# Blocks 8 to 11 as one group of four in an attention and two-layer kernel: second layer by seven products, weights' sums placed earlier, start and end reordered

## The chip, the cores and the metric

The kernel runs on one core of a Trainium2 chip. The metric is device time in microseconds (us) of one execution, the median over several runs. Everything below that names an engine uses the profile's short names: PE is TensorE (matrix products; PEld is its loading of weights), DVE is VectorE, ACT is ScalarE, POOL is GpSimd, SP is SyncE, which here only issues transfers.

## The reference

A sliding-window attention whose scores decay with distance is followed by a normalisation and two matrix layers with a residual. B, H, S, D are 8, 8, 576 and 64; the model width is 512, the hidden width 2048. The kernel computes in half precision with single-precision sums.

```python
scores = scale * np.matmul(q, k.transpose(0, 1, 3, 2))
...
bias = slopes[:, None, None] * (-np.abs(rel).astype(np.float32))[None, :, :]
mask = (rel >= 0) & (rel < window)          # window = 128
scores = np.where(mask, scores + bias[None], -1000000000.0)
...
attn = attn / (np.sum(attn, axis=-1, keepdims=True) + 1e-09)
x = np.matmul(attn, v)                      # then heads side by side: B, S, H * D
mu = np.mean(x, axis=-1, keepdims=True)
var = np.mean((x - mu) ** 2, axis=-1, keepdims=True)
xn = (x - mu) / np.sqrt(var + 1e-06) * g_ln
ch = np.maximum(xn @ w_ch1, 0.0) @ w_ch2
return (x + ch).astype(np.float32)
```

## The kernel before, in words

**Blocks and groups.** Two batches make a pair, and the tokens of a pair are cut into nine blocks of 128 tokens (the ninth, T, holds the two tails of 64). Four pairs give 36 blocks, numbered 0 to 35 in `order`. Attention runs block by block. The two layers run over groups of consecutive blocks: `GROUPS` says how many blocks each group has, six groups of two and then six of four (line 26). A group's input is the normalised x of its blocks, transposed, in one tile `xT`; its hidden values lie in one tile `ht`.

**Attention steps.** The list `steps` (lines 654 to 705) holds small pieces of attention. From block 8 on, each block n has four: (1) the values of block n (`values`, two halves on TensorE, each followed by a reciprocal and a scaling on VectorE, lines 473 to 510) and the scores of block n+2 (`attend`, matmuls and one exponential on ACT per half, lines 407 to 449); (2) the masks of block n+2 (two multiplications on VectorE, line 454) and the statistics of block n (`stats`: two instructions on VectorE, then two on GpSimd that give the reciprocal deviation, lines 536 to 542); (3) `turn`, the transposing of queries and keys for a later pair of blocks: for the first three pairs TensorE transposes into the banks of the scores and VectorE and ACT copy out (lines 326 to 336), for the last a transfer does it; (4) `normal`, which centres and scales block n on VectorE and then has SP issue a transposing transfer into `xT` (lines 522 to 534). Loads from memory are issued on GpSimd's queue, ahead of the values (`load_until`, lines 266 to 271); GpSimd's two arithmetic instructions of a block stand in the same queue.

**First layer.** `mlp1` (lines 719 to 750) has 16 units; a unit is four matmuls into one bank and one rectification on ACT (on VectorE for the units listed in `on_dve`). With two blocks a matmul has 256 columns, with four 512.

**Second layer, two ways.** `mlp2` (lines 752 to 772) is the plain way: 16 matmuls of 512 columns per block, summed in one bank, which `finish` adds to x on VectorE (line 903) and stores. `fast_mlp2` (lines 798 to 898), for groups from `FAST` on, splits hidden, weights and output into quarters and computes the group by seven products instead of eight. It needs sums of quarters of the weights, made once by `combine_w2` (lines 178 to 192, eight instructions on VectorE, the last two of which overwrite weights that the plain way reads), and sums of quarters of hidden, made for each group by `combine_hidden` (lines 783 to 796): four instructions after the first layer's unit 10, four more within the products. Each product is 8 matmuls of 256 columns for each of two pairs of blocks; eight additions (`add`, line 845) gather the products, and `send` stores a pair of blocks. A product's bank can be written again only after its addition.

**Banks.** Four banks of the accumulator serve the layers and the values; two double ones serve the scores and the transposes. From the fast groups on the four are a `ring` handed out in turn (`psum`, lines 377 to 385); within `fast_mlp2` two are set aside and two (`others`) serve the values, the second product and the last.

**What sets the order.** The order on TensorE, SP, ACT and VectorE is that of the program text, written by hand: `weave_at` (lines 926 to 930) runs the units of a layer and, after unit u, as many attention steps as u stands in its list of places; after the units in `also` it emits one of the eight weights' sums. The lists are at lines 947 to 966. An instruction that waits holds up all that follow on its engine. Before the first layer begins, single warm products (`warm`, lines 278 to 283) fill TensorE's time.

Of the kernel before, what the change touches and what calls it, by code (L numbers as in the profile page):

```python
# [24 lines left out]
HALF = P // 2  # L25
GROUPS = [2] * 6 + [4] * 6
FAST = 6

# [31 lines left out]
def kernel(  # L60
# [246 lines left out]
    def turn(p, i, in_sc=False, copies=(nc.vector.tensor_copy, nc.scalar.copy)):  # L307
# [19 lines left out]
        if i < 4:  # L327
            transposed("q", p, i, [t[:, 0] for t in ps])
            transposed("k", p, i, [t[:, 1] for t in ps])
            for b, copy in enumerate(copies):  # L330
                copy(out=q[:, b], in_=ps[b][:, 0])
                copy(out=k[:, b].rearrange("p h (c r) -> p r h c", r=2), in_=ps[b][:, 1])
        else:
            for tag, t, dst, copy in zip("qk", ps, (q, k), copies):
                transposed(tag, p, i, [t[:, 0]])
                copy(out=dst[:, 0].rearrange("p h (c r) -> p r h c", r=2), in_=t[:, 0])
# [288 lines left out]
    def turn_step(n, *how):  # L625
        p, blk = order[n]
        return [(turn, p, blk // 2) + how]
# [22 lines left out]
    def warm_step(n):  # L650
        return [[(warm, n)]]
# [4 lines left out]
    steps += values_steps(0)  # L656
    steps += [turn_step(2, True, (nc.scalar.copy, nc.scalar.copy))]
    steps += values_steps(1) + warm_step(4)
# [33 lines left out]
    for n in range(8, count):  # L692
# [4 lines left out]
        if n + 2 < count:  # L697
            step += scores_step(n + 2)
        steps.append(step)
        steps.append(  # L700
            [m for t in (n + 1, n + 2) if t < count for m in masks_of(t)] + [(stats, n)]
        )
        if n + 1 < count:
            steps.append(turn_at(n + 1))
        steps.append([(normal, n)])
    combined = combine_w2()
# [11 lines left out]

    def mlp1(g, on_dve=()):
        xT = turned_x[g]  # L720
        w = w1 if g < FIRST_GROUPS else w1g
        cols = len(members[g]) * P
        ht = hidden[g] = hidden_pool.tile([P, NFB, 4 * P], FP16, tag="ht", name="ht")
        turn_about = chain(*zip(range(QF), range(QF, NFB)))
        for u, fb in enumerate(turn_about if g >= FAST else range(NFB)):
# [21 lines left out]
            yield cols  # L747
            if g >= FAST and u == 10:
                for i in range(4):
                    combine_hidden(g, 0, i)  # L750
# [47 lines left out]
    def fast_mlp2(g):  # L798
# [77 lines left out]
        add("z", 0, 1, False)  # L876
        send(0)
        yield DM
        yield from product("x", s[2], t3, False)
        add("x", 1, 0, True)  # L880
        add("x", 1, 1, False)
        if use["w"][0] is use["w"][1]:
# [6 lines left out]
        else:  # L889
            low, high = slice(0, QD), slice(QD, DM)  # L890
            last = product("w", a[1][1], t4, True)
            send(1, cols=high, queues=(nc.sync, nc.scalar))
            yield DM
# [50 lines left out]
    with tc.manual_schedule(engines={engine.PE, engine.SP}):  # L944
        with tc.manual_schedule(engines={engine.Activation, engine.DVE}):
# [4 lines left out]
            weave_at(mlp2(1), 0, 1, 2, 3, 4, 6, 6)  # L950
            weave_at(mlp1(2), 0, 3, 3, 6, 8, 11)
            weave_at(mlp2(2), 0, 2, 4, 6, 7)


            weave_at(mlp1(3, (9, 10, 11)), 8, 8, 12, 13)
            weave_at(mlp2(3), 0, 1, 1, 3, 4, 4, 5, 6)
            weave_at(mlp1(4), 0, 4, 8, 10, 10, 14)
            weave_at(mlp2(4), 0, 2, 2, 5, 5, 7, also=(1, 4, 6))
            weave_at(mlp1(5), 0, 5, 5, 8, 10, 12, also=(3, 6, 9))
            weave_at(mlp2(5), 0, 1, 2, 4, 6, 7)  # L960
            ring += [ps_mm.tile([P, DM], FP32, tag="mm", name="ps_r") for _ in range(4)]
            for g in range(6, len(GROUPS)):
                weave_at(
                    mlp1(g), 0, 2, 5, 7, 8, 10, 13, 15, also=(1, 4) if g == 6 else ()
                )
                weave_at(fast_mlp2(g), 1, 3, 6, 7, 7, 10, 12, 13)
# [31 lines left out]
```

## Time and profile before

| what | us |
|---|---|
| three runs | 318.67, 319.58, 320.78 |
| median | 319.58 |
| the profiled execution, its own time | 320.09 |
| its span in the profile | 318.3 |
| first layer of blocks 8 and 9 begins | 96.18 |
| their plain second layer begins | 106.84 |
| first layer of blocks 10 and 11 begins | 116.68 |
| their plain second layer begins | 126.93 |
| first layer of blocks 12 to 15 begins | 136.82 |
| their seven products begin | 153.18 |
| last matmul's record ends, last issue of a store, span ends | 313.4, 315.24, 318.3 |

The profile is of one execution; its span is the time from the first to the last instruction, and the execution's own time holds some more around it. A group of the profile stands under a line of the kernel, an engine and an operation, with the tiles written and read. Of the matmuls the starts are exact and the ends modelled, so the pace of a row of them is read from the starts. Times inside the span count from its start.

### The profile page before, as it was taken

The page shows a single profiled execution, that of the slowest core. Times are in us where ns is not written, and L with a number is a line of the kernel's source. Part 1 is how long each engine was busy: PE and PEld are TensorE (multiplying, and loading weights), DVE is VectorE, ACT ScalarE, POOL GpSimd, SP SyncE. Part 2 cuts the span into 40 slices and gives each one's busy share as a digit, 9 for nine tenths or more (in the row PEclk, how much of TensorE's full clock was granted, in tenths as well). Part 3 has the DMA queues.
Part 4 walks back from the last instruction along what each step waited for, and adds up shares of the span by engine and source line. Part 5 has one row for each costly group of instructions (what it writes and reads, how often), then busy time and mean ns, then how long its engine had stood idle before and what let it go on. Part 6 is the DMA issues. An engine that isn't in the chain of part 4 may idle for free.

```text
span 318.3 us, 9920 instructions
## 1 busy us (share of the span) xinstructions
PE 304.7 (96%) x4190; PEld 205.4 (65%) x4190; DVE 228.9 (72%) x547; ACT 179.4 (56%) x311; POOL 124.7 (39%) x196
## 2 busy tenths in 40 slices
PE   7789999999898999999999999999999999999993
PEld 3468755757656657555885588558855874784583
DVE  2769977878667699767995889469948995761462
ACT  6578774757647558459437832772487247305600
POOL 8922769557245365483345472240001001100000
PEclk9989999999999999999999999999999999999999
DMA  9999999999986979499949994893347244015005
GB/s 112 165 206 197 190 151 182 198 110 146 106 95 91 116 87 161 52 153 62 77 51 146 181 124 52 134 156 64 83 91 127 18 84 85 19 36 114 0 0 135
DMA packets 121183, 34.68 MB, mean 109 GB/s; under 512 B 112049, under 2 KB 116785, under 8 KB 121138
## 3 DMA queue, kind: packets, MB, share of 16 engines
q0 software_dynamic: 89216, 18.36, 70.5%
q1 hardware_dynamic: 31602, 15.42, 25.6%
q8 instruction: 33, 0.54, 0.7%
q10 hardware_dynamic: 320, 0.26, 0.4%
q14 instruction: 12, 0.10, 0.1%
HBM read 36.90 MB, written 9.44 MB: 146 GB/s over the span
## 4 chain that ended last, share of the span: by engine, by line
PE 84%; DVE 5%; POOL 3%; ACT 2%; DMA 2%; issue 2%; POOLq 0%; ACTq 0%
PE ps_r L728 26%; PE ps_r L827 23%; PE ps_m L761 11%; PE ps_m L728 10%; PE ps_sc L434 5%; PE ps_r L487 3%; PE ps_sc L301 2%; PE ps_pv L487 2%; ACT probs L443 2%; DMA k<-in_k_dram 2%; POOL q L237 1%; DVE o L903 1%; DVE x L496 1%; PE ps_warm L283 1%; DVE probs L454 1%
## 5 line engine op out<-in xcount | busy, mean ns | idle before, releaser
L728 PEld LDWEIGHTS <-w1g 128*128 128x128 f16 x640 | 60.4, 98 | 50.5 <-DVE x L496 1.8
L728 PE MATMUL ps_r<-xT,w1g 128*128 128x512 f16 x384 | 85.1, 379 | 0.0
L443 ACT ACTIVATE probs<-ps_sc 128x1024 f16<-128x1024 f32 x56 | 54.2, 1021 | 52.3 <-PE ps_sc L434 52.3
L744 ACT ACTIVATE ht<-ps_r 128x512 f16<-128x512 f32 x96 | 56.2, 600 | 31.6 <-PE ps_r L728 31.5
L761 PE MATMUL ps_m<-w,ht 128*128 128x512 f16 x192 | 46.0, 380 | 1.2 <-ACT ht L744 1.2
L539 POOL TENSOR_TENSOR rstd<-moments,powers 128x1 f32<-128x1 f32 x28 | 6.8, 243 | 102.4 <-DVE moments L585 102.4
L827 PE MATMUL ps_r<-w,ht 128*128 128x256 f16 x384 | 44.1, 273 | 0.0
L454 DVE TENSOR_TENSOR probs<-probs,m 128x1024 f16<-128x1024 f16 x56 | 37.5, 688 | 8.7 <-ACT probs L443 8.5
L247 POOL DMA_DIRECT2D vx<-in_v_dram x40 | 34.7, 884 | 22.3 <-PE ps_r L487 9.0
L827 PEld LDWEIGHTS <-ht 128*128 128x128 f16 x384 | 37.1, 98 | 4.8
L744 ACT ACTIVATE ht<-ps_m 128x256 f16<-128x256 f32 x91 | 32.9, 391 | 8.6 <-PE ps_m L728 6.2
L728 PE MATMUL ps_m<-xT,w1g 128*128 128x256 f16 x256 | 31.5, 273 | 2.2 <-DVE x L496 0.9
L761 PEld LDWEIGHTS <-ht 128*128 128x128 f16 x192 | 17.1, 98 | 18.7 <-issue 1.3
L237 POOL DMA_DIRECT2D q<-in_q_dram x30 | 20.5, 692 | 19.3 <-PE ps_sc L301 10.6
L584 DVE BATCH_NORM_STATS2 st<-x 128x6 f32<-128x512 f16 x36 | 24.6, 685 | 0.0
L237 POOL DMA_DIRECT2D k<-in_k_dram x30 | 20.2, 686 | 4.8 <-DMA w<-in_moe_w_ch_dram 3.5
L434 PE MATMUL ps_sc<-q,k 64*64 64x128 f16 (+1 forms) x1088 | 20.5, 210 | 1.5 <-ACT probs L443 1.1
L827 PE MATMUL ps_r<-w,hs 128*128 128x256 f16 x192 | 21.9, 273 | 0.0
L487 PEld LDWEIGHTS <-probs 128*128 128x128 f16 x448 | 18.8, 97 | 4.7 <-DVE probs L454 0.3
L827 PEld LDWEIGHTS <-hs 128*128 128x128 f16 x192 | 18.8, 98 | 2.2
L845 DVE TENSOR_TENSOR o<-ps_r,x 128x512 f32<-128x512 f32 x24 | 16.5, 686 | 4.3 <-PE ps_r L827 4.3
L434 PEld LDWEIGHTS <-k 64*64 64x64 f16 x1088 | 15.2, 108 | 6.8 <-issue 4.6
(87 smaller groups left out, 381.4 us busy)
## 6 DMA issues: line engine op xcount, KB each, us to landing
out_dram<-o SPq DMA_DIRECT2D x68, 128.0 KB, 2.9
k<-in_k_dram POOLq DMA_DIRECT2D x32, 128.0 KB, 6.0
vx<-in_v_dram POOLq DMA_DIRECT2D x32, 128.0 KB, 6.0
w<-in_moe_w_ch_dram POOLq DMA_DIRECT2D x8, 512.0 KB, 9.4
q<-in_q_dram POOLq DMA_DIRECT2D x24, 128.0 KB, 4.2
q<-in_q_dram POOLq DMA_DIRECT2D x24, 64.0 KB, 3.8
k<-in_k_dram POOLq DMA_DIRECT2D x8, 64.0 KB, 4.8
vx<-in_v_dram POOLq DMA_DIRECT2D x8, 64.0 KB, 5.0
```

Of the source, the lines that this page charges most:

```text
L237: nc.gpsimd.dma_start(out=t[b * n // 2 : (b + 1) * n // 2], in_=src[2 * p + b, :, i * P : i * P + n, :].rearrange("h (c r) d -> c h r d", ...
L247: nc.gpsimd.dma_start(out=vx[p0 : p0 + n, :, 0:D], in_=v[b, :, t0 : t0 + n, :].rearrange("h p d -> p h d"),)
L434: nc.tensor.matmul(in_halves(ps[cols, j, n, t, :])[:, r, queries], kt[rows, hp, cols], in_halves(qt[rows, b, hp])[:, r, queries], start=Tr ...
L443: nc.scalar.activation(out=dst.rearrange("p (n j) q -> p j n q", j=2), in_=ps.rearrange("p j n t q -> p j n (t q)"), func=AF.Exp, scale=in ...
L454: nc.vector.tensor_tensor(out=dst, in0=dst, in1=mask, op=ALU.mult)
L487: nc.tensor.matmul(ps[:, i, :], pr[:, h, t, :], vext[(p * NSLOT + o) % NV][:, h, :], start=(n == 0), stop=(n == len(terms) - 1),)
L584: nc.vector.bn_stats(out=st, in_=xs[order[n]])
L728: nc.tensor.matmul(ps[:, 0:cols], w[:, kb, fb * P : (fb + 1) * P], xT[:, kb, 0:cols], start=(kb == 0), stop=(kb == NKB - 1),)
L744: nc.scalar.activation(out=ht[:, fb, 0:cols], in_=ps[:, 0:cols], func=AF.Relu)
L761: nc.tensor.matmul(sums[at], ht[:, fb, at * P : (at + 1) * P], w2[:, fb, :], start=(fb == 0), stop=(fb == NFB - 1),)
L827: nc.tensor.matmul(banks[name][pair][:, pair, :], lhs[:, fb, pair * P : (pair + 1) * P], rhs[:, fb, :], start=(first and fb == 0 and (pair ...
L845: nc.vector.tensor_tensor(out=o[:, at, cols], in0=banks[name][at.start][:, at, :], in1=(x if to_x else o)[:, at, cols], op=ALU.add,)
```

## The change

`GROUPS` becomes four groups of two and seven of four, and `FAST` goes from 6 to 4: blocks 8 to 11, two groups before, are one group. Its first layer runs in two halves, each over two blocks with matmuls of 256 columns, the halves writing the two sides of one hidden tile; sums of hidden are taken after unit 10 of the second half. Its second layer is the seven products.

The 24 attention steps that lay around the two groups' layers lie around the new group's: 5 in the first half, 7 in the second, 12 in the products (the other groups of four have 8 and 8). For block 11 (`HURRIED`) the statistics come before the masks and the centring before the transposing of queries and keys.

The eight weights' sums move: one into the first layer of blocks 4 and 5, two into their second, one into the first layer of blocks 6 and 7, two into their second, and two into the first half of the new group. Before, they lay in the layers of blocks 8 to 11 (six) and in the first layer of blocks 12 to 15 (two).

At the start, two warm products go before the transposes of block 2 and three between its queries' and its keys'. At the end, the last group's first send alternates between the queues of SP and ACT; in all fast groups the addition of the second pair's high columns comes before that of its low columns, and in the last group the store of the high columns stands between them.

The diff:

```diff
-GROUPS = [2] * 6 + [4] * 6
-FAST = 6
+GROUPS = [2] * 4 + [4] * 7
+FAST, HURRIED = 4, 11
...
             transposed("q", p, i, [t[:, 0] for t in ps])
+            if p == 0 and i == 1:
+                warm(3)
             transposed("k", p, i, [t[:, 1] for t in ps])
...
-    steps += [turn_step(2, True, (nc.scalar.copy, nc.scalar.copy))]
+    steps += warm_step(2) + [turn_step(2, True, (nc.scalar.copy, nc.scalar.copy))]
...
-        steps.append(
-            [m for t in (n + 1, n + 2) if t < count for m in masks_of(t)] + [(stats, n)]
-        )
-        if n + 1 < count:
-            steps.append(turn_at(n + 1))
-        steps.append([(normal, n)])
+        to_mask = [m for t in (n + 1, n + 2) if t < count for m in masks_of(t)]
+        turns = [turn_at(n + 1)] if n + 1 < count else []
+        if n == HURRIED:
+            steps += [[(stats, n)] + to_mask, [(normal, n)], *turns]
+        else:
+            steps += [to_mask + [(stats, n)], *turns, [(normal, n)]]
...
-    def mlp1(g, on_dve=()):
+    def mlp1(g, on_dve=(), part=0, parts=1):
...
-        cols = len(members[g]) * P
-        ht = hidden[g] = hidden_pool.tile([P, NFB, 4 * P], FP16, tag="ht", name="ht")
+        cols = len(members[g]) * P // parts
+        if part == 0:
+            hidden[g] = hidden_pool.tile([P, NFB, 4 * P], FP16, tag="ht", name="ht")
+        xT, ht = (t[:, :, part * cols : (part + 1) * cols] for t in (xT, hidden[g]))
...
-            if g >= FAST and u == 10:
+            if g >= FAST and part == parts - 1 and u == 10:
...
-        send(0)
+        send(0, queues=(nc.sync, nc.scalar) if g == len(GROUPS) - 1 else (nc.sync,))
         yield DM
         yield from product("x", s[2], t3, False)
+        add("x", 1, 1, False)
+        low, high = slice(0, QD), slice(QD, DM)
+        if g == len(GROUPS) - 1:
+            send(1, cols=high, queues=(nc.sync, nc.scalar))
         add("x", 1, 0, True)
-        add("x", 1, 1, False)
...
-            low, high = slice(0, QD), slice(QD, DM)
             last = product("w", a[1][1], t4, True)
-            send(1, cols=high, queues=(nc.sync, nc.scalar))
...
-            weave_at(mlp1(2), 0, 3, 3, 6, 8, 11)
-            weave_at(mlp2(2), 0, 2, 4, 6, 7)
-            weave_at(mlp1(3, (9, 10, 11)), 8, 8, 12, 13)
-            weave_at(mlp2(3), 0, 1, 1, 3, 4, 4, 5, 6)
-            weave_at(mlp1(4), 0, 4, 8, 10, 10, 14)
-            weave_at(mlp2(4), 0, 2, 2, 5, 5, 7, also=(1, 4, 6))
-            weave_at(mlp1(5), 0, 5, 5, 8, 10, 12, also=(3, 6, 9))
-            weave_at(mlp2(5), 0, 1, 2, 4, 6, 7)
+            weave_at(mlp1(2), 0, 3, 3, 6, 8, 11, also=(14,))
+            weave_at(mlp2(2), 0, 2, 4, 6, 7, also=(3, 5))
+            weave_at(mlp1(3, (9, 10, 11)), 8, 8, 12, 13, also=(5,))
+            weave_at(mlp2(3), 0, 1, 1, 3, 4, 4, 5, 6, also=(2, 6))
             ring += [ps_mm.tile([P, DM], FP32, tag="mm", name="ps_r") for _ in range(4)]
-            for g in range(6, len(GROUPS)):
-                weave_at(
-                    mlp1(g), 0, 2, 5, 7, 8, 10, 13, 15, also=(1, 4) if g == 6 else ()
-                )
+            weave_at(mlp1(4, (), 0, 2), 0, 3, 5, 10, 13, also=(2, 8))
+            weave_at(mlp1(4, (), 1, 2), 0, 0, 4, 8, 10, 12, 15)
+            weave_at(fast_mlp2(4), 0, 3, 4, 5, 7, 7, 7, 8, 10, 11, 12, 13)
+            for g in range(5, len(GROUPS)):
+                weave_at(mlp1(g), 0, 2, 5, 7, 8, 10, 13, 15)
                 weave_at(fast_mlp2(g), 1, 3, 6, 7, 7, 10, 12, 13)
```

## The prediction

> **What bounds the kernel now.** I read the page first, then the chain of waits in order of time, then TensorE's and VectorE's timelines around blocks 8 to 11, the busy times by stage, and the queues at both ends. The page:
>
> ```profile
> span 318.3 us, 9920 instructions
> PE 304.7 (96%) x4190; PEld 205.4 (65%) x4190; DVE 228.9 (72%) x547; ACT 179.4 (56%) x311; POOL 124.7 (39%) x196
> PE 84%; DVE 5%; POOL 3%; ACT 2%; DMA 2%; issue 2%; POOLq 0%; ACTq 0%
> ```
>
> TensorE sets the end; from 137 us on the chain holds nothing else but the last addition. The chain in order of time (start, length, what):
>
> ```profile
> 96.02 0.57 POOL rstd L542
> 96.61 0.41 DVE xc L526
> 97.15 0.42 DVE x L496
> 97.77 0.28 issue
> 98.04 0.75 DVE o L903
> 98.84 1.03 PE ps_m L728 x8
> ...
> 107.00 2.59 PE ps_m L761 x12
> ...
> 301.14 12.24 PE ps_r L827 x112
> ```
>
> Where the first layer of blocks 8 and 9 begins, TensorE waits for VectorE, whose queue stands behind GpSimd's reciprocal deviation. The last two lines price the second layer: 2.59/12 = 0.216 us per plain product of 512 columns, and 12.24 us for the 112 of seven products. Busy times by stage:
>
> ```profile
> core 0: us, PE busy (x) PEld busy (x) DVE busy (x) ACT busy (x) POOL busy (x), PEclk, DMA share, GB/s
> 136.80:152.70 15.90, 15.90 (x188) 7.94 (x186) 11.14 (x25) 12.88 (x21) 10.13 (x16) 1.00 1.34 106
> 152.70:168.40 15.70, 15.70 (x305) 13.85 (x306) 15.23 (x33) 5.59 (x8) 6.00 (x11) 1.00 0.84 67
> ```
>
> First layer, then seven products, of the first fast group (blocks 12 to 15). In the products VectorE is busy 15.23 of 15.70 us and still holds nobody up; it carries eight steps of attention there. Its timeline gives the price of its instructions by their starts, 0.60 each, 0.72 and 0.10 for statistics:
>
> ```profile
> 155.14 0.69 DVE L845 TENSOR_TENSOR o<-ps_r,x 128x512 f32<-128x512 f32 x1
> 155.75 0.68 DVE L796 TENSOR_TENSOR w<-ht,hs 128x1024 f16<-128x1024 f16 x1
> 156.35 1.29 DVE L454 TENSOR_TENSOR probs<-probs,m 128x1024 f16<-128x1024 f16 x2
> 157.55 0.69 DVE L584 BATCH_NORM_STATS2 st<-x 128x6 f32<-128x512 f16 x1
> 158.27 0.18 DVE L585 BATCH_NORM_AGGREGATE moments<-st 128x2 f32<-128x6 f32 x1
> ```
>
> The ends: granted clock by stretch, and the last issues of the two queues.
>
> ```profile
> 11.05:14.47 3.42, 1.83 (x79) 1.40 (x80) 2.81 (x10) 0.41 (x2) 3.07 (x6) 1.00 2.00 161
> 14.47:17.88 3.41, 3.41 (x29) 1.47 (x29) 2.11 (x8) 2.78 (x5) 2.12 (x4) 0.50 1.23 199
> 17.88:21.29 3.41, 2.33 (x81) 1.89 (x74) 1.87 (x5) 3.08 (x4) 1.15 (x2) 1.00 1.24 207
> ```
>
> ```profile
> 310.63 3.03 SPq L922 DMA_DIRECT2D out_dram<-o  x5
> 313.70 0.77 SPq L918 DMA_DIRECT2D out_dram<-o  x1
> 314.57 0.55 SPq L922 DMA_DIRECT2D out_dram<-o  x1
> 315.24 0.55 SPq L918 DMA_DIRECT2D out_dram<-o  x1
> ```
>
> After 14.47 us the clock is half for 3.41 us. At the end five issues stand in one queue, so the last comes at 315.24 though its data is ready at 313.83.
>
> **The change part by part.** All times are of the profiled execution.
>
> *Second layer.* 64 products of 512 columns (13.81) become 112 of 256 (12.24): **-1.57**. The first layer keeps its 128 matmuls of 256 columns. Its waits change: before, 0.51, 0.12 and 0.10 at 117.64 to 118.74 (banks held by a plain sum), 0.14 at 122.5, and 0.41 and 0.47 behind ACT's two exponentials; after, only the last kind, once per half: **-0.93**. Bounds 0 and -1.75.
>
> *Weights' sums sooner*, eight of 0.60 on VectorE. One falls into its wait of 1.74 us before 66.80, two into 0.28 and 1.00 before 73.19 and 74.89, one into 1.67 before 81.37: nothing, and with that cover gone 0.6 each. The fifth and sixth fall between 91.8 and 98.8, the chain shown above: the fifth delays the statistics of block 10, GpSimd's answer, and the values of block 11; the sixth stands before L903, which frees the fourth bank. The first layer's fourth unit starts at 100.03 instead of 98.84: **+1.19**. Bounds 0 (if GpSimd's wait of 0.95 and a bank more took them) and 1.2. The last two stand in the first half.
>
> *Second half's input.* Block 11's x is centred after its statistics (100.72), two masks (101.92), a weights' sum (102.52): done at 102.85. SP issues its DMA transpose about 0.1 later. Such a transpose took 2.4 to 7.4 us to land; block 11's took 6.0 (102.20 to 108.24), with the q and k loads in flight that GpSimd sends right after the same reciprocal deviation, as it will. So it lands at 109.0. TensorE is through the first half at 106.84 + 1.19 = 108.0: **+1.0**, bounds 0 (the median of 3.8) and 2.5. Before, this input had until 116.7.
>
> *VectorE in the products.* The stage gets twelve steps of attention in place of eight. From the copy of block 17's queries, which TensorE releases at 114.9 (without the 1.0), VectorE has no free place up to the last product's addition: 8 sums of hidden (5.2), 8 additions (4.8), 6 masks (3.6), values of blocks 14 to 16 at 1.1 (3.3), 3 statistics at 0.82 (2.46), 4 centrings at 0.33 (1.3), copies of queries and keys (0.63 + 2 x 0.95), and the GpSimd answer for block 15, whose centring stands right behind its statistics (0.95); with 0.2 for a product not yet done it is 24.4 us, to 139.3. On the way the values of block 15 wait for the bank of the second product, the scores of 17 for a bank that VectorE copies out. Before, from the fourth unit (98.84) to the second unit of the next group (137.68) TensorE took 38.84 us, 1.75 of it the waits above; 38.84 - 1.75 - 1.57 = 35.5 us of work are left. From 100.03 on, with two ACT waits (0.82) and the 1.0, it would reach that unit at 137.4; but the unit needs the last addition's bank, free at 139.4 + 1.0 = 140.4: **+3.0**. Bounds 0 (the stage before hid 15.23 in 15.70) and 4.0 (GpSimd's longest, 1.86, in place of 0.95). I take 3.0, as VectorE's queue is summed from its own rows. The middle is 140.4 - 137.7 = **+2.7**.
>
> *Order in moved steps.* Eight stores of blocks 8 to 11, 0.6 us each on SP, now come at the end of the products and ahead of block 16's and 17's transposes, which TensorE needs over 15 us later: nothing, and 4.8 if it did. Loads keep their order on GpSimd. The swapped additions cost nothing where all groups but the last are concerned, as nobody waits between them.
>
> *Start.* Two warm products before block 2's transposes and three between its q and k fall into waits of 0.42, 0.23 and 0.79 for loads; k lands at 13.83 in any case. They add 1.08 us to a stretch with 1.83 busy; 2.33 was enough at 17.88. So the clock stays, and four warm products end at 15.4 instead of 16.2. Then ACT's copies bind: block 0's copy at 16.5, the first exponential at 17.1 instead of 18.21: **-1.1**. The first quarter of weights landed at 18.03, the next at 20.54 and 23.07, each before its use even so. Bounds -1.2 and +0.7 (five at 427 ns less the waits' 1.44).
>
> The Trainium skill (TensorE: Matmul & The Clock Gate, What's actually happening) says that the clock is gated by a free-running window of 3413 ns that a kernel's start does not reset. The 3.41 us above agree in length; no run here shows another phase. By that rule a median execution may not have had the slow stretch at all, and this term would be 0, and the time 321.4.
>
> *End.* Half of the first send goes to ACT's queue, and the addition for the high columns comes first, done at 312.35. Each queue then has four issues at 0.62 to 0.69 as ACT's had (312.98, 313.60, 314.29, 314.94): the last at about 314.4 instead of 315.24: **-0.85**, bounds -1.0 (data ready at 313.83) and 0. The landing about 2 us later stays.
>
> Sum: -1.57 - 0.93 + 1.19 + 1.0 + 3.0 - 1.1 - 0.85 = +0.74. The profiled execution took 320.09 us (its span 318.3 and 1.8 around it, which nothing here changes), 0.51 over the median of 319.58; 320.09 + 0.74 = 320.8, and by the median **320.3**.
>
> **Rivals.**
> - *VectorE holds nobody up in the products* (the 3.0 goes, the rest stays): 320.3 - 3.0 = 317.3. For it: the stage before hid 97% busy. Against: twelve steps instead of eight.
> - *The saving comes whole* (1.19 and 1.0 go too): 317.3 - 2.2 = 315.1. Against: the chain at 96 to 98.8 has no place for two sums.
> - *The change does not do at the start what it says:* the clock falls all the same, or was up already: 320.3 + 1.1 = 321.4. For it: the three times shown differ by 2.1 us. The Trainium skill's free-running window (TensorE: Matmul & The Clock Gate, What's actually happening) would do this.
> - *Slower:* the transpose of block 11, behind the loads, decides. Each us over 6.0 from issue to landing is a us of TensorE's. At 7.4, the longest shown, the time is 321.7; slower by over 1% from 8.5. For it: the queue's landings of 6.0 and 7.4 came beside loads; against: the median of 3.8.
>
> **How the numbers follow.** A measurement of this kernel can hardly tell less than 1% (3.2 us) from no change: faster is under 316.4, slower over 322.8. Forecast as summed 0.47 (own range 319.1 to 321.7); VectorE keeps up 0.17; whole saving 0.06; no gain at the start 0.15; late transpose 0.15. Faster: the whole saving and a corner of the first rival, 0.08. Slower: the transpose's upper half and the forecast's tail, 0.10. Same: 0.82. The range from 316.9 to 322.4 leaves out the whole saving, the lower edge of the first rival, and the slower cases, 0.2 in all.
>
> **What would show it.** Right: granted clock 1.00 from 4.2 us on and the first exponential near 17.1; TensorE's fourth unit of the first half waiting for L903; a wait for xT at the second half; VectorE over 97% busy in blocks 8 to 11's products and TensorE waiting there and at the next group's second unit for L845; the last issue 0.9 us sooner after the last product. Wrong: no TensorE wait between 108 and 140 us, or the next fast group's start earlier than before by over 2 us.

## The result, and the profile after

| | us |
|---|---|
| after, median of 22 runs (lowest to highest) | 321.47 (320.14 to 324.13) |
| before, median of 22 runs on the same chip | 319.57 (318.26 to 321.85) |
| ratio | 1.0060, 95% interval 1.0042 to 1.0078 |
| profiled execution of after, and its span | 321.24, 319.5 |

The change costs 0.6%, 1.9 us. The two profiled executions differ by 1.15 us (321.24 and 320.09), since that of before lies 0.5 us above its median and that of after 0.2 below. Line numbers after the change are some four higher (a sum's addition is L849, the plain way's addition L908, a plain first-layer matmul L732, a product's L831).

The page of after: TensorE is 1.5 us less busy, VectorE 5.9 us more, and VectorE's share of the chain that ended last went from 5% to 11%.

```profile
span 319.5 us, 10054 instructions
...
PE 303.2 (95%) x4243; PEld 210.2 (66%) x4243; DVE 234.8 (73%) x559; ACT 179.8 (56%) x311; POOL 125.1 (39%) x196
...
PE 76%; DVE 11%; POOL 3%; DMA 3%; ACT 3%; issue 3%; DVEq 0%; POOLq 0%; ACTq 0%
```

Busy times by stage in after: the two stretches at the start whose second had a granted clock of 0.50 before, then the products.

```profile
core 0: us, PE busy (x) PEld busy (x) DVE busy (x) ACT busy (x) POOL busy (x), PEclk, DMA share, GB/s
11.05:14.47 3.42, 2.40 (x56) 1.10 (x59) 3.06 (x10) 0.56 (x1) 3.06 (x5) 1.00 2.02 166
14.47:17.88 3.41, 3.24 (x84) 2.02 (x84) 2.13 (x9) 3.00 (x6) 2.12 (x3) 1.00 1.25 205
119.13:139.17 20.04, 17.43 (x372) 14.49 (x369) 18.45 (x41) 8.65 (x11) 9.29 (x17) 1.00 1.08 98
```

TensorE's timeline in after (start, length, line, count, and in brackets the idle time in front and who ended it):

```profile
97.71 1.16 PE L732 MATMUL ps_r<-xT,w1g 128*128 128x256 f16 x8 [1.78 <-DVE x L498]
99.51 1.47 PE L732 MATMUL ps_r<-xT,w1g 128*128 128x256 f16 x12 [0.65 <-DVE o L908]
...
107.06 2.78 PE L732 MATMUL ps_r<-xT,w1g 128*128 128x256 f16 x24 [0.25 <-ACT ht L748]
...
124.43 0.64 PE L489 MATMUL ps_r<-vx,probs 128*128 128x65 f16 x16 [0.35 <-DVE o L849]
...
126.00 0.41 PE L436 MATMUL ps_sc<-q,k 64*64 64x128 f16 x16 [0.58 <-DVE k L334]
...
137.31 1.02 PE L732 MATMUL ps_r<-xT,w1g 128*128 128x512 f16 x4 [0.85 <-DVE o L849]
139.17 1.02 PE L732 MATMUL ps_r<-xT,w1g 128*128 128x512 f16 x4 [0.83 <-DVE o L849]
```

The bracket understates what a wait costs, as the ends of matmuls are modelled. By the starts (the distance to the matmul before, less the usual pace of 0.110 us for 256 columns and 0.216 for 512) the rows lose 1.94, 0.81, 0.41, 0.51, 0.78, 1.05 and 1.00 us; such losses are meant below. The last four, 3.34 us, are TensorE waiting for VectorE within and right after the products. In before TensorE waits nowhere for VectorE from 119 us on. The first layer's second half (from 107.5 on) waits for no input. VectorE's timeline at the end of the products shows why the last two wait:

```profile
134.58 0.68 DVE L456 TENSOR_TENSOR own<-own,m 128x1024 f16<-128x1024 f16 x1
135.19 0.68 DVE L586 BATCH_NORM_STATS2 st<-x 128x6 f32<-128x512 f16 x1
135.90 0.18 DVE L587 BATCH_NORM_AGGREGATE moments<-st 128x2 f32<-128x6 f32 x1
136.00 0.66 DVE L849 TENSOR_TENSOR o<-ps_r,o 128x512 f32<-128x512 f32 x1
136.58 0.68 DVE L849 TENSOR_TENSOR o<-ps_r,x 128x512 f32<-128x512 f32 x1
137.18 0.41 DVE L333 COPY q<-ps_sc 128x512 f16<-128x512 f16 x1
137.51 0.72 DVE L334 COPY k<-ps_sc 128x512 f16<-128x512 f16 x1
138.12 0.40 DVE L528 TENSOR_SCALAR xc<-x,moments,rstd 128x512 f16<-128x512 f16 x1
138.43 0.68 DVE L849 TENSOR_TENSOR o<-ps_r,o 128x512 f32<-128x512 f32 x1
```

No idle time stands in front of any of these rows: VectorE works without a pause, and the last addition, which frees a bank of the next group, comes after masks, statistics, copies and a centring of attention. Its product was long ready: the last matmul of it starts at 135.12, 3.3 us ahead of the addition.

The last issues of SP and of ACT in after, one fence each:

```profile
314.36 0.60 SPq L923 DMA_DIRECT2D out_dram<-o  x1
315.06 0.54 SPq L927 DMA_DIRECT2D out_dram<-o  x1
315.70 0.54 SPq L923 DMA_DIRECT2D out_dram<-o  x1
```

```profile
314.39 0.85 ACTq L923 DMA_DIRECT2D out_dram<-o  x1
315.34 0.56 ACTq L927 DMA_DIRECT2D out_dram<-o  x1
316.00 0.55 ACTq L923 DMA_DIRECT2D out_dram<-o  x1
```

The last matmul starts at 314.57 (before 313.10), so the last issue follows it by 1.43 us instead of 2.14.

Between the two profiles the time went so: start -0.67 (first layer from 20.13 instead of 20.81), middle +2.16 (the next fast group's second unit at 139.17 instead of 137.68, over and above the start), nothing from there to the last matmul, end -0.3. The gain at the end stands in the other profiles too: from the last matmul's start to the end of the span it takes 4.6 to 4.9 us in the ten usable profiles with the changed end, and 5.2 to 5.4 in the three without.

One disturbed execution each of steps_later (616.5 us) and of copies_sums (325.73 us) is left out of the medians below, and as that of steps_later is the profiled one, only the times of that kernel are used.

### The profile page after: what moved, and what is told of

The parts are those of the page before. It is cut to its first block, busy times and chain, and to the rows that moved or that the text cites. A ratio compares the mean times of both kernels' runs of the same rounds, so it can differ in the third digit from the quotient of the medians.

```text
span 319.5 us, 10054 instructions
## 1 busy us (share of the span) xinstructions
PE 303.2 (95%) x4243; PEld 210.2 (66%) x4243; DVE 234.8 (73%) x559; ACT 179.8 (56%) x311; POOL 125.1 (39%) x196
## 4 chain that ended last, share of the span: by engine, by line
PE 76%; DVE 11%; POOL 3%; DMA 3%; ACT 3%; issue 3%; DVEq 0%; POOLq 0%; ACTq 0%
PE ps_r L732 28%; PE ps_r L831 23%; PE ps_m L732 7%; PE ps_m L765 6%; PE ps_sc L436 4%; PE ps_r L489 3%; DMA k<-in_k_dram 2%; DVE o L849 2%; PE ps_sc L301 2%; ACT probs L445 2%; DVE probs L456 2%; DMA q<-in_q_dram 1%; DVE x L498 1%; POOL q L237 1%; PE ps_pv L489 1%
## 5 line engine op out<-in xcount | busy, mean ns | idle before, releaser
L732 PE MATMUL ps_r<-xT,w1g 128*128 128x512 f16 (+1 forms) x512 | 100.9, 353 | 4.8 <-DVE x L498 1.8
L732 PEld LDWEIGHTS <-w1g 128*128 128x128 f16 x640 | 60.7, 98 | 52.6 <-issue 3.8
L748 ACT ACTIVATE ht<-ps_r 128x512 f16<-128x512 f32 (+1 forms) x128 | 67.2, 549 | 36.9 <-PE ps_r L732 35.0
L831 PE MATMUL ps_r<-w,ht 128*128 128x256 f16 x448 | 51.6, 273 | 0.0
L831 PEld LDWEIGHTS <-ht 128*128 128x128 f16 x448 | 43.2, 98 | 5.6
L765 PE MATMUL ps_m<-w,ht 128*128 128x512 f16 x128 | 31.2, 380 | 1.2 <-ACT ht L748 1.2
L748 ACT ACTIVATE ht<-ps_m 128x256 f16<-128x256 f32 x59 | 22.3, 385 | 6.6 <-PE ps_m L732 4.6
L831 PE MATMUL ps_r<-w,hs 128*128 128x256 f16 x224 | 25.8, 273 | 0.0
L831 PEld LDWEIGHTS <-hs 128*128 128x128 f16 x224 | 21.8, 98 | 2.6
L849 DVE TENSOR_TENSOR o<-ps_r,o 128x512 f32<-128x512 f32 (+1 forms) x29 | 18.8, 658 | 5.0 <-PE ps_r L831 4.9
L497 DVE RECIPROCAL rec<-ps_r 128x4 f32<-128x4 f32 x48 | 8.4, 174 | 18.1 <-PE ps_r L489 18.1
L498 DVE SCALAR_TENSOR_TENSOR x<-ps_r,rec 128x256 f16<-128x256 f32 x48 | 20.4, 424 | 1.7
L849 DVE TENSOR_TENSOR o<-ps_r,x 128x512 f32<-128x512 f32 x28 | 19.2, 685 | 2.6 <-PE ps_r L831 2.5
```

Source lines behind the costliest of these rows:

```text
L732: nc.tensor.matmul(ps[:, 0:cols], w[:, kb, fb * P : (fb + 1) * P], xT[:, kb, 0:cols], start=(kb == 0), stop=(kb == NKB - 1),)
L748: nc.scalar.activation(out=ht[:, fb, 0:cols], in_=ps[:, 0:cols], func=AF.Relu)
L765: nc.tensor.matmul(sums[at], ht[:, fb, at * P : (at + 1) * P], w2[:, fb, :], start=(fb == 0), stop=(fb == NFB - 1),)
L831: nc.tensor.matmul(banks[name][pair][:, pair, :], lhs[:, fb, pair * P : (pair + 1) * P], rhs[:, fb, :], start=(first and fb == 0 and (pair ...
L849: nc.vector.tensor_tensor(out=o[:, at, cols], in0=banks[name][at.start][:, at, :], in1=(x if to_x else o)[:, at, cols], op=ALU.add,)
```

## The experiments

Twelve kernels, each against the kernel before on its own chip. "us" is the ratio's distance from 1 times 319.5; on this scale after stands at +1.9.

| kernel | median | ratio, 95% interval | us |
|---|---|---|---|
| start_only | 319.28 | 1.0006, 0.9985 to 1.0027 | +0.2 |
| end_only | 318.57 | 0.9980, 0.9956 to 1.0005 | -0.6 |
| middle_only | 321.16 | 1.0074, 1.0043 to 1.0105 | +2.4 |
| plain_second | 320.36 | 1.0035, 1.0008 to 1.0062 | +1.1 |
| sums_aside | 320.08 | 1.0032, 1.0006 to 1.0059 | +1.0 |
| steps_later | 326.25 | 1.0226, 1.0193 to 1.0258 | +7.2 |
| sums_steps | 324.40 | 1.0175, 1.0146 to 1.0203 | +5.6 |
| steps_tail | 323.77 | 1.0139, 1.0104 to 1.0174 | +4.4 |
| tail_sums | 321.62 | 1.0069, 1.0043 to 1.0095 | +2.2 |
| no_masks | 319.49 | 0.9998, 0.9977 to 1.0018 | -0.1 |
| no_masks_sums | 316.99 | 0.9940, 0.9919 to 0.9960 | -1.9 |
| copies_sums | 318.80 | 0.9982, 0.9951 to 1.0014 | -0.6 |

### The three parts of the change, one at a time

**start_only**: the kernel before with the five warm products.

```diff
             transposed("q", p, i, [t[:, 0] for t in ps])
+            if p == 0 and i == 1:
+                warm(3)
...
-    steps += [turn_step(2, True, (nc.scalar.copy, nc.scalar.copy))]
+    steps += warm_step(2) + [turn_step(2, True, (nc.scalar.copy, nc.scalar.copy))]
```

> The kernel before with the five warm products at the start alone. The theory of the prediction (the clock falls before, and stays up with them): 1.1 us faster by the sum, 0.7 us by the profile after, where the second k tile landed 0.5 us later. Rival (the slow clock was a matter of that execution's phase, other executions before did not have it): within 0.3 us of before. A second rival (the warm products themselves hold the transposes up): slower by up to 0.7 us. In the profile: granted clock 1.00 between 14.5 and 17.9 us by all three, so the times decide; the first exponential of block 2 near 17.1 to 17.5.

**end_only**: the kernel before with the changed end.

```diff
-        send(0)
+        send(0, queues=(nc.sync, nc.scalar) if g == len(GROUPS) - 1 else (nc.sync,))
...
+        add("x", 1, 1, False)
+        if g == len(GROUPS) - 1:
+            send(1, cols=high, queues=(nc.sync, nc.scalar))
         add("x", 1, 0, True)
-        add("x", 1, 1, False)
...
-            low, high = slice(0, QD), slice(QD, DM)
             last = product("w", a[1][1], t4, True)
-            send(1, cols=high, queues=(nc.sync, nc.scalar))
```

> The kernel before with the changed end alone. By the sum 0.85 us faster. By the profile after: the last issue 0.7 us sooner after the last matmul, but 0.4 us of it lost between the last landing and the end of the span, so 0.3 us faster. Rival (the tail is bound by the landing of the last store, however it is issued): no difference.

**middle_only**: the changed kernel with start and end as before (both diffs above, undone).

> The changed kernel with the start and the end as before: the group of four, the sums' places and the steps alone. By the sum 2.7 us slower than before, by the profile after 2.2 us (no wait for the transposed input). If the two ends do nothing, it is 1.9 us slower like the changed kernel itself; if they give what the sum said, it is 3.8 us slower.

The three add up: 0.2 - 0.6 + 2.4 = 2.0, against 1.9 for the whole. The middle costs what the whole costs, the end gives 0.6 (its interval reaches from -1.4 to +0.2), and the start gives nothing that can be measured, though the profile of start_only shows the clock up where that of before has 0.50:

```profile
11.05:14.47 3.42, 3.08 (x87) 1.72 (x87) 3.06 (x11) 0.83 (x2) 3.33 (x6) 1.00 2.14 161
14.47:17.88 3.41, 2.66 (x48) 1.50 (x45) 2.06 (x9) 3.41 (x7) 1.87 (x3) 1.00 1.23 197
```

and its first layer of blocks 8 and 9 begins at 95.31 instead of 96.18. The first exponential of block 2 comes at 16.79 us there, at 17.48 in after and at 18.21 in before, so in the profiles the mechanism is the one that was forecast.

What the profiles show there does not hold for the median. Each execution comes with its mean granted clock; one stretch of 3.41 us at half of 318 us makes 0.9946. The fall of the clock after the last matmul, which costs nothing, takes off up to 0.004 in these profiles (start_only's has 0.996 from that alone). So an execution with a mean of 0.996 or more has no room for a slow stretch. Of 105 other executions of before, 77 are of this kind; 20 lie below 0.9945, and their median is 320.54, against 318.97 for the 85 above (the 48 at 0.998 or more have 319.03). So most executions of before had no costly slow stretch that warm products could take away.

What the warm products do to those that had one is less clear. The profiles of all three kernels with the start of before (before, end_only, middle_only) have the slow stretch, between 14.5 and 23.4 us; none of the ten with the warm products and a record of the clock has one before 130 us. Yet the mean still falls below 0.9945 with them, in two of start_only's twelve executions and in 7 of 22 of after (median 322.2; the 10 at 0.998 or more have 320.8). The mean does not say where in an execution the clock was low, so whether these had it at the start isn't shown.

### The second layer and the weights' sums

**plain_second**: the changed kernel with the group of four, but its second layer the plain way, its layers ahead of the ring of banks and the last two weights' sums in the next first layer.

```diff
-FAST, HURRIED = 4, 11
+FAST, HURRIED = 5, 11
...
-            weave_at(mlp1(4, (), 0, 2), 0, 3, 5, 10, 13, also=(2, 8))
+            weave_at(mlp1(4, (), 0, 2), 0, 3, 5, 10, 13)
...
-            weave_at(fast_mlp2(4), 0, 3, 4, 5, 7, 7, 7, 8, 10, 11, 12, 13)
+            weave_at(mlp2(4), 0, 3, 4, 6, 7, 8, 9, 9, 11, 12, 14, 15)
```

> The changed kernel with the group of blocks 8 to 11 in its place, but its second layer in the plain way (64 products of 512 columns, four sums) with the same twelve steps beside it; the last two weights' sums go to the first layer of the next group. VectorE loses 16 instructions of 0.6 us there and gains 4 of 0.65. Theory (VectorE's queue sets the end of that stage, 3.3 us): TensorE takes 1.57 us more and waits 3.3 us less, so 1.7 us faster than the changed kernel, equal to before within 0.5 us. Rival (the first half and the sums cost it, the products save what they should): 1.6 us slower than the changed kernel, 3.5 us slower than before.

0.8 us faster than the whole change, where the theory had 1.7 and the rival 1.6 slower; with an interval of about 1 us on such a difference the times alone leave the sign open. The profile is clearer: with 64 products of 512 columns in place of 112 of 256, but without the eight sums of hidden and with four additions in place of eight on VectorE, TensorE waits for VectorE nowhere in the second layer, and right after it once, for 0.47 us. From the start of the first layer's second half to the next fast group's second unit it takes 30.48 us, against 31.67 in after. So by the profiles the seven products lose more than they save here. This run also shows the late input that after's profile does not have; TensorE's timeline in plain_second:

```profile
106.17 0.60 PE L732 MATMUL ps_m<-xT,w1g 128*128 128x256 f16 x4 [0.25 <-ACT ht L748]
108.06 2.34 PE L732 MATMUL ps_m<-xT,w1g 128*128 128x256 f16 x20 [1.29 <-DMA xT<-xc]
```

Block 11's transpose was issued at 101.86 and landed 6.07 us later, a loss of 1.45 us. In middle_only it took 5.45 us (issued at 103.87, loss 0.50); in after, issued at 102.41, 4.62, and nobody waited.

**sums_aside**: the changed kernel with the fifth and sixth weights' sums in the layers of blocks 6 and 7.

```diff
-            weave_at(mlp1(3, (9, 10, 11)), 8, 8, 12, 13, also=(5,))
-            weave_at(mlp2(3), 0, 1, 1, 3, 4, 4, 5, 6, also=(2, 6))
+            weave_at(mlp1(3, (9, 10, 11)), 8, 8, 12, 13, also=(5, 6))
+            weave_at(mlp2(3), 0, 1, 1, 3, 4, 4, 5, 6, also=(0,))
```

> The changed kernel with the fifth and sixth weights' sums taken out of the stretch between 91 and 99 us: one to VectorE's wait before 81.4 us, one to its wait before 88.1 us. Theory (each delayed block 11's values or the fourth bank by its 0.6 us, 1.2 us of TensorE's): 1.2 us faster than the changed kernel, 0.7 us slower than before; in the profile the first half's fourth unit starts 1.2 us sooner. Rival (the time is given back, because VectorE is late in the products anyway and the stage's end is set there): no faster than the changed kernel by more than 0.3 us.

0.9 us faster than the whole change, by times that could not tell it from the rival's 0.3. TensorE's timeline in sums_aside: one wait where after has two.

```profile
94.57 0.60 PE L732 MATMUL ps_r<-xT,w1g 128*128 128x256 f16 x4 [0.21 <-DMA xT<-xc]
96.19 2.67 PE L732 MATMUL ps_r<-xT,w1g 128*128 128x256 f16 x20 [1.02 <-DVE x L498]
```

The 0.81 for the fourth bank fell to 0.21, which before has too, and the wait ahead of it from 1.94 to 1.19; the four waits of the products stay as they were (0.52, 0.78, 1.05, 1.00), so by the profile the gain is not given back.

### Moving steps out of the products

**steps_later**: eight of the twelve attention steps in the products, twelve in the next first layer. **sums_steps**: the same with the sums aside.

```diff
-            weave_at(fast_mlp2(4), 0, 3, 4, 5, 7, 7, 7, 8, 10, 11, 12, 13)
+            weave_at(fast_mlp2(4), 1, 3, 6, 7, 7, 10, 12, 13)
...
+                if g == 5:
+                    weave_at(mlp1(g), 0, 1, 3, 4, 5, 7, 9, 10, 11, 12, 14, 15)
+                else:
+                    weave_at(mlp1(g), 0, 2, 5, 7, 8, 10, 13, 15)
```

> The changed kernel with eight steps of attention beside the seven products of blocks 8 to 11 instead of twelve; the other four go to the first layer of blocks 12 to 15, which gets twelve. Theory (VectorE is 3.3 us behind in the products because of these steps): TensorE's four waits between 124 and 140 us go, some of it comes back in the next first layer, where ACT has two exponentials more: 2 to 3.3 us faster than the changed kernel, 0 to 1.4 us faster than before. Rival (VectorE is late from the first half on, whatever stands beside the products): less than 1 us faster than the changed kernel.

> Both of the last two together on the changed kernel. If the two waits are independent: 3.2 to 4.5 us faster than the changed kernel, that is 316.9 to 318.3 where before takes 319.6. If the second gives back the first: as the version with eight steps alone.

Both miss by far, but neither tests the theory: the lists also move the centring of block 15 from after unit 7 to after unit 12 of the products, and so the transfer that fills the next group's input. TensorE's timeline in sums_steps:

```profile
136.74 3.57 PE L732 MATMUL ps_r<-xT,w1g 128*128 128x512 f16 x8 [4.95 <-DMA out_dram<-o]
```

It loses 5.15 us before the next group's first matmul. SP issued the transpose at 132.23, between stores. The bracket names a store, but the stores ahead of the transpose had landed by 133.94 and those behind it landed at 136.85 and later, when the matmul had begun; the transpose landed at 136.63, 4.4 us after its issue, and is what TensorE waited for. The clock fell at 133.74 and stays at 0.50 until 140.57 (from the first of the eight matmuls to the one behind them it takes 3.50 us, where 1.73 is usual at full clock). All six executions of sums_steps have a mean clock of 0.987 to 0.989; the profiled one has 0.988. The four waits of the products are gone in this run. That steps_later, with the same lists, waits for the same transfer is likely, but no usable profile shows it. The lists changed two things at once; the next experiment moves only one.

**steps_tail**: only the last four of the twelve move (statistics, turning and centring of block 16 and the values of block 17; the expectation has the values of block 16 in place of the last), block 15's centring stays. **tail_sums**: the same with the sums aside.

```diff
-            weave_at(fast_mlp2(4), 0, 3, 4, 5, 7, 7, 7, 8, 10, 11, 12, 13)
+            weave_at(fast_mlp2(4), 0, 3, 4, 5, 7, 7, 7, 8)
...
+                    weave_at(mlp1(g), 0, 1, 3, 4, 5, 7, 9, 10, 11, 12, 14, 15)
```

> The changed kernel with only the last four of the twelve attention steps in the products of blocks 8 to 11 (values, statistics, turning and centring of block 16) moved into the next group's first layer, which gets twelve; block 15's centring stays where it is. Theory (VectorE's queue of 24.4 us in the products sets the next group's second unit): VectorE has some 4 us less ahead of the last additions, so TensorE's waits of 0.85 and 0.83 at 137 to 139 us go (2.05 us lost there), those at 124 to 126 stay (1.3): 319.4, 2.0 us faster than the changed kernel and the same as the one before. Rival (the waits come from the additions' banks whatever else VectorE does): waits stay, 321.4. Second rival: twelve steps in a first layer cost there what they cost in the products: waits for VectorE within that first layer, 321.4 or more.

> The changed kernel with both repairs: the four steps moved as in the run beside it, and the fifth and sixth weights' sums placed earlier (into the layers of blocks 6 and 7), as in the earlier run that gained 0.9 us. Theory, where the two costs are separate waits on TensorE: 321.4 - 2.0 - 0.9 = 318.5, below the kernel before by 0.8 us. Rival: the two waits hide behind each other (VectorE's queue is late whenever TensorE is early): no faster than the better of the two alone, 319.4.

2.5 us slower than the whole change instead of 2.0 faster: the second rival. The losses at the end of the products fall from 2.05 to 0.63 us, and a new one of 2.31 stands at the end of the next first layer. TensorE's timeline, then VectorE's, in steps_tail:

```profile
152.43 0.42 PE L489 MATMUL ps_r<-vx,own 128*128 128x65 f16 x8
155.00 0.63 PE L436 MATMUL ps_sc<-q,k 64*64 64x128 f16 x32 [2.15 <-DVE k L334]
```

```profile
151.29 0.68 DVE L800 TENSOR_TENSOR ht<-ht 128x1024 f16<-128x1024 f16 x1
151.89 1.29 DVE L456 TENSOR_TENSOR probs<-probs,m 128x1024 f16<-128x1024 f16 x2
153.10 0.69 DVE L586 BATCH_NORM_STATS2 st<-x 128x6 f32<-128x512 f16 x1
153.82 0.18 DVE L587 BATCH_NORM_AGGREGATE moments<-st 128x2 f32<-128x6 f32 x1
153.92 0.39 DVE L333 COPY q<-ps_sc 128x512 f16<-128x512 f16 x1
154.23 0.72 DVE L334 COPY k<-ps_sc 128x512 f16<-128x512 f16 x1
```

The moved work stands here behind the next group's sums of hidden, and the scores wait for the copy at its end. By the two profiles steps_tail takes 0.95 us more than after; the medians say 2.5. Its six executions have a median granted clock of 0.992 (after 0.9965), which may be a part of the rest; where the clock fell isn't shown, and the rest stays open. tail_sums has the same new wait (1.26 us) and one of 1.80 for the transposed input of the next group. It takes 2.2 us less than steps_tail and about as long as the whole change (0.3 more), where 318.5 was expected.

### Taking work off VectorE

**no_masks** and, with the sums aside as well, **no_masks_sums**: both leave out six mask multiplications, and so do not compute the reference's function.

```diff
-        todo = unmasked.get((p, blk), [])
+        todo = [] if (p, blk) in ((1, 7), (1, T), (2, 0)) else unmasked.get((p, blk), [])
```

> The changed kernel with the six mask multiplications left out that VectorE has within the products of blocks 8 to 11 (those of blocks 16, 17 and 18, so the weights of these blocks stay unmasked; nothing else is moved, and no other engine's work changes). Theory (VectorE's queue in the products is what TensorE waits for): 6 x 0.60 = 3.6 us less on it, the four waits at 124 to 139 us (3.34 us lost in the profile of the changed kernel) go, the waits of 0.4 and 0.5 for ACT stay: 321.4 - 3.3 = 318.1. Rival (the waits are those of the products' banks and their order, not of the length of VectorE's queue): waits stay, 321.4. Second rival: the work left over on VectorE binds at the next place where it binds now, as in the run with the four steps moved, and at most half comes back: 319.8.

> The same with the fifth and sixth weights' sums placed earlier as well (masks of blocks 16 to 18 left out again). Theory, where the change's own saving of matmuls is real and only VectorE's two queues ate it: 318.1 - 0.9 = 317.2, faster than the kernel before by 0.6%, near the 317.3 that the prediction gave where VectorE holds nobody up (that figure still holds the weights' sums and the late input). Rival (the time comes back at the next wait, the transposed input of the second half or of the next group): 318.1 or more.

With 3.6 us less on VectorE, 2.0 us come back by the times (319.49, 1.4 over the 318.1 of the theory, between it and the second rival's 1.7 us at most) and 2.6 by the profile: of the four waits one is left, so the profile speaks for the theory and the times leave room for a part of the rival. TensorE's timeline in no_masks:

```profile
97.62 1.16 PE L732 MATMUL ps_r<-xT,w1g 128*128 128x256 f16 x8 [1.41 <-DVE x L498]
99.42 1.47 PE L732 MATMUL ps_r<-xT,w1g 128*128 128x256 f16 x12 [0.65 <-DVE o L908]
...
136.66 5.56 PE L732 MATMUL ps_r<-xT,w1g 128*128 128x512 f16 x25 [0.55 <-DVE o L849]
```

No row between 124 and 135 has a wait; the one that is left loses 0.71 us. With the sums aside too the time is 316.99, 1.9 us below the kernel before and 0.2 off the 317.2 expected. A part of the 1.9 may be the changed end's (0.6 in end_only, which its interval does not tell from nothing); by the profile the stretch from the first layer's start to the next fast group's second unit takes 115.33 us, against 116.88 in before. So the saving of matmuls is real, and VectorE's two queues, at 98 to 99 us and at 124 to 139, ate it. The kernel before was not run without these masks; as TensorE waits nowhere for VectorE there, its masks should cost nothing, but no run shows it. The sums were worth 0.9 us alone, 1.9 here and 2.2 between steps_tail and tail_sums, each give or take 1 us or more; in the profiles the two waits at 97 to 99 us shrink by 1.35, 1.1 and 1.1.

**copies_sums**: the changed kernel, nothing left out, with two pairs of copies moved from VectorE to ACT, and the sums aside.

```diff
-            for f in turn_step(m, True)
+            for f in turn_step(m, True, *[(nc.scalar.copy,) * 2] * (m in (18, 20)))
```

> The changed kernel, nothing left out, with VectorE relieved in two ways: the copies of queries and keys for blocks 18 and 20, which it makes within the products of blocks 8 to 11 (2 x 0.95 us), go to ACT, which there does another 1.33 us of copies and an exponential at a time and stands idle in between; and the fifth and sixth weights' sums are placed earlier. Theory (VectorE's queue there is what TensorE waits for): of the 3.34 us of waits in the products about 1.9 go, most of them at 126 and at 137 to 139 us, and 0.9 at 98 to 99 us: 321.4 - 1.9 - 0.9 = 318.6, below the kernel before by about 0.8 us. Rival (the copies only move: TensorE now waits for ACT's copies before the next scores, 1.3 us each time): 320.5, the weights' sums' gain alone.

2.5 us faster than the change as made, and 0.2 off the 318.6 expected; against before it is 0.6 us faster, which its interval does not tell from no difference. By the profile the stretch from the first layer's start to the next fast group's second unit takes 116.89 us, as in before (116.88): the middle now costs nothing, and gains nothing. TensorE's timeline in copies_sums: no wait at 126, one at the end as long as in after and one shorter (1.04 and 0.59 us by the starts, where after loses 1.05 and 1.00).

```profile
123.07 0.64 PE L489 MATMUL ps_r<-vx,probs 128*128 128x65 f16 x16 [0.36 <-DVE o L849]
123.64 0.63 PE L436 MATMUL ps_sc<-q,k 64*64 64x128 f16 x32
...
135.18 1.02 PE L732 MATMUL ps_r<-xT,w1g 128*128 128x512 f16 x4 [0.84 <-DVE o L849]
136.63 5.56 PE L732 MATMUL ps_r<-xT,w1g 128*128 128x512 f16 x25 [0.43 <-DVE o L849]
```

1.2 of the 3.34 us went, not 1.9: once the copies are off it, VectorE idles 0.44 us for GpSimd's reciprocal deviation at 135.57, between two additions, where in after it came late for it.

## Why the prediction was right, and where it was not

320.3 was forecast, 321.47 measured: inside the range, within 1%, 1.2 us over. Term by term, in us (the first five terms make up the middle, 0.2 of which by the profile falls to none of them):

| term | predicted | profile of after against before | times |
|---|---|---|---|
| second layer, 112 for 64 | -1.57 | -1.5 (112 at 0.110) | |
| waits in the first layer | -0.93 | -0.82 | |
| fifth and sixth weights' sums | +1.19 | +1.34 | +0.9, 1.9, 2.2 (three pairs) |
| second half's input | +1.0 | 0 (0.50 and 1.45 in two other profiles) | |
| VectorE in the products | +3.0 | +3.34 | at least +2.0 (no_masks) |
| middle | +2.7 | +2.16 | +2.4 (middle_only) |
| start | -1.1 | -0.67 | +0.2, within 0.7 (start_only) |
| end | -0.85 | -0.3 | -0.6, within 0.8 (end_only) |
| sum | +0.74 | +1.15 | +1.9 |

- *VectorE's queue in the products* was the step that carried the forecast, and it held in its mechanism, its size and its place: TensorE waits for L849 at the next group's first two units, the last addition starts at 138.43, and taking 3.6 us off VectorE takes three of the four waits away. The rival in which VectorE holds nobody up (317.3) is out for the kernel as changed; with the masks left out and the sums aside it is 316.99. The marker "over 97% busy" was wrong: 18.45 of 20.04 us are 92%, since 0.37 us of waiting for TensorE and 0.95 for GpSimd lie in the stretch. What sets the end is the order of the queue, not its share.
- *The weights' sums* held as well: the fourth unit starts 1.34 us late, waiting for L908, and moving the two sums gives it back.
- *The second half's input* was a price taken from one landing of 6.0 us, with the loads of queries and keys as its reason. After the change the transpose landed after 4.62 us, in seven of the other changed kernels after 4.45 to 4.70, in middle_only after 5.45 and in plain_second after 6.07. The loads are issued at the same distance from it in all of them, so they do not make the difference; what does isn't shown. 0 is what this profile shows. The rival "slower", a landing over 7.4 us, did not occur.
- *The start* failed, and it is most of the 1.2 us. In the profiles the term is there in part: in after the first exponential comes 0.73 us sooner, not 1.1, as the rest of block 2's keys landed 0.5 later (TensorE goes on at 14.40 instead of 13.88). But the step "the clock stays, so -1.1" took a slow stretch of one profiled execution for a property of the kernel, and 77 of 105 executions of before have a mean clock that leaves no room for it. The rival that said the clock falls all the same, or was up already, gave 321.4, and that is the time; "was up already" is what the clocks show for most executions. The Trainium skill (TensorE: Matmul & The Clock Gate, What's actually happening) says that the gate's window runs freely and that the cold stretch differs between runs of one kernel; the trace agrees: the clock first rose at 4.23, 5.55, 4.5, 4.35, 6.38, 7.38 and 6.49 us in seven profiles, and each stretch at half clock in an early stage lasted 3.41 us.
- *The end* was right in its mechanism (two queues, the last issue 1.43 instead of 2.14 us after the last matmul's start, 0.71 of the 0.85). In the profile 0.4 of it is lost again: from the last landing (318.01 us) to VectorE's next record it takes 0.84 us instead of 0.44. Why isn't shown.

The forecast's sum came out 1.2 us low because the two terms that were gains, start and end, were by the times 1.3 and 0.25 too large (by the profile 0.43 and 0.55); the middle, where the reasoning was, was within 0.6. The middle's closeness holds some luck: the late input, forecast at 1.0, did not come in this profile, and part of it was made up by the other terms of the middle, each of which cost 0.1 to 0.3 more than forecast.

## What to carry to other kernels

A way to compute that takes matmuls away and adds work to the engine beside TensorE is priced by that engine's queue, summed in order up to the instruction that frees the next bank, and not by busy shares: here 1.57 us were saved and 3.34 lost to additions that stood behind masks, statistics and copies. Moving such work later helps only if the later place is not the next such queue; moving it to an engine that idles there (two pairs of copies to ACT, 1.2 us of waits) does. A gain that hangs on the granted clock at one place of one profile should be held against the clocks of the other executions before it enters a sum.

## What the runs showed of the hardware

- The clock fell after stretches with no long pause. In the 3.41 us ahead of the early slow stretch TensorE was busy for 1.83 us in before, 2.19 in end_only and 1.97 in middle_only, and its longest wait there was 0.79 us in before. The Trainium skill (TensorE: Matmul & The Clock Gate, Why this matters for your kernels) advises against idle gaps over some 3 us; here, many short ones were enough. The busy time alone does not decide, though: from 94.31 to 97.72 us after has only 1.57 us busy, and the clock stays at 1.00. The stretches that brought it down hold mostly short matmuls of attention (79 matmuls in before), the one that did not 9 of the layers, of 256 and 512 columns; whether that is the reason isn't shown.
- In all thirteen profiles with a record of the clock the times between its changes are multiples of 3.41 us, from 1 (3.41) over 4 (13.65) to 92 (314.03).
- A wait that takes TensorE through such a stretch costs more than itself: after the 5.15 us in sums_steps eight matmuls took 3.50 us instead of 1.73, and executions of the kernel before with a mean clock below 0.9945 took 1.6 us longer than the others.
- A transposing transfer of one block from SP, issued in the same place of the program with the same loads behind it, landed after 4.45 to 7.36 us in thirteen profiles. Fifteen of the sixteen signals that tell of its landing had come after 4.3 to 4.7 us in every one of them; where the transfer was late (before, start_only, end_only, middle_only, plain_second), it was the last one alone that came 1.0 to 3.0 us behind.
